# One adaLN block on one core: modulation and Q,K weights loaded without doubled rows, the late modulation in groups of four tiles, another written-out order

## The chip, the cores and the metric

One core of a Trainium2 chip runs the whole program. The metric is the device time of one execution in microseconds (us), the median of several. TensorE (PE) multiplies matrices; VectorE (DVE), ScalarE (ACT) and GpSimd (POOL) work elementwise; SyncE (SP) issues most DMA transfers, ACT a few. Each engine takes its instructions in the order in which the program lists them for it, and waits on semaphores for the others.

## What is computed

x has 2048 rows of 448. Six vectors come from c; then an attention with 16 heads of 28 over a sliding window of 256 rows, and a gated MLP with a mixing over the rows:

```
mod = (silu(c) @ w_mod).reshape(1, 6, 1, 448)         # sa, ca, ga, sb, cb, gb
h = layernorm(x) * (1 + ca) + sa
q, k, v = split(h @ wqkv)                              # 16 heads of 28
p = softmax(where(0 <= i - j < 256, q k^T * 28**-0.5, -1e9))
x = x + ga * ((p v) @ wo)
h = layernorm(x) * (1 + cb) + sb
z = gelu(h @ w_in); z1 = z[:, :896]; z2 = layernorm(z[:, 896:])
x = x + gb * ((z1 * (w_sp @ z2 + b_sp)) @ w_out)
```

## The kernel before

The 2048 rows are 16 tiles of 128. The 448 features lie in four chunks of 128 that start at 0, 128, 192 and 320 (`CH`), so features 192 to 255 stand in chunk 1 and in chunk 2. `load_dup` (L481) loads a weight to match: rows 0 to 255 into chunks 0 and 1, rows 192 to 447 into chunks 2 and 3, which is 512 rows for 448. The doubled rows must count once: for Q and K a memset (`z_qk`, L528) zeroes the lower 64 partitions of chunk 2, for the modulation a zero in the row of c (`z_c`, L539) does it.

Every step is an operation with a name, made by `P.op`. The text ORDER lists all operations by their place in that list; a number may carry a PSUM bank choice (after a slash) and an engine choice (after a dot). `schedule` (L81) takes them in that order, and `emit` (L115) writes each engine's instruction stream from it, with the semaphore waits that follow from the data, from a buffer's last users and from the PSUM banks. So ORDER sets every engine's order, SP's and ACT's transfers among them. The names used below, in order of work:

- Loads: `c`; `x0`, `x0b`, `x1` to `x4` (tiles 0; 1; 2-3; 4-7; 8-11; 12-15); `wmodA` (columns of sa and ca); `wqk` (Q and K columns); `wv`; `wmodG` (ga); `woq0` to `woq2` (wo).
- Start: `silu0` loads ACT's first table, `c_cols` turns c into columns, `silu` makes `sc_sb`, `modA` are 16 pairs of one-column matmuls, and `modAe` (DVE, L574) puts sa and 1+ca into `modT`. `warm` are 22 matmuls without use.
- First LayerNorm: `l1_t st0` and `ag` are the statistics of tile t (DVE, L589, L592), `ve`, `rs` (POOL, L597) and `nm` its scale and shift, `xn t` the normalized tile. Tiles are taken in blocks: block 0 is tile 0, block 1 tile 1, block 2 tiles 2-3, blocks 3 to 5 four tiles each. Blocks 0 to 2 are transposed by PE (`tr`), and `hT b_u` (L673 on ACT, L678 on DVE) applies `modT` while it empties the bank; blocks 3 to 5 go through DMA transposes (`hx t`, L695) and four modulating operations each (`hm b_c`, L687).
- Q and K weights: heads of 28 columns are spread to 32 by `wqkf0_c`, `wqkf1_c` (c the chunk, 0 or 1 for the first or second half of the heads; L710 to L712). `qk b_g` are the projections, four matmul steps each, g 0 to 3 for Q and 4 to 7 for K; in block 0 four of the eight read the unspread weights (`mm_heads`, L751). `qke b_g` empties them (L783 ACT, L786 DVE); `v t` and `ve t` are the same for V (L795, L798).
- Attention of tile j: `S j_u` scores, `E j_u` the exponential of 1024 columns (ACT, L885), `M j_u` the mask (POOL, L891), `PV j_u`, `oq`, `rec`, `nrm`, `oT` (L917 to L926), `wo j`, and `x1_j` adds to x (L936). For tile 0 the scores come in two halves, `S0_0h0` and `S0_0h2`, each with two pairs of banks: (0,1),(2,3) and (4,5),(6,7). `E0_0` and `E0_1` read them.
- Second LayerNorm: `l2_j` as above in pairs of tiles, `x2_j` (L610), DMA transpose `h2T j`, and four modulating operations of 256 columns per pair, `h2m j_c` (L945 to L957).
- MLP: `z2m t` and `z1m tb_f` are the projections with w_in. Five tiles (0 to 4) are done early: `z2e` copies them (L983, L986) and `z2g` applies gelu later; the others go through gelu directly (`z2g`, `z1g`). `l3` and `z2n` normalize z2. `G` multiplies with w_sp (loaded transposed, `wsp`), `ga`, `gu`, then `out`, `fin` and the store `st`.

The S of tile j+1 is listed ahead of the PV of tile j, and the PSUM banks 0 to 5 rotate in pairs among the S. The last `E15_5` comes after `z1g0_5`, `z1g0_4` and `z2g7`.

## Time and profile before

| | us |
|---|---|
| median of 3 runs | 271.01 (270.79 to 271.61) |
| profiled execution | 270.71 |
| its span in the trace | 268.7 |
| PE busy | 256.8 (96%) |
| DVE busy | 172.5 (64%) |
| ACT busy | 133.3 (50%) |
| POOL busy | 106.6 (40%) |

The span runs from the first instruction to the last; the execution's time has 2.0 us more around it. In the timeline a row has start, duration, engine, line, operation, tiles, shape, count, and in brackets the idle time of the engine before it with what ended it. Rows of the same kind in sequence are merged, and then the duration is that of all of them with the small gaps between. ACT operations overlap, so 60 E of 1044 ns stand in 55.80 us.

### The profile page before, as it was taken

What the parts mean: (1) busy time and instruction counts of PE and PEld (TensorE: products, weight loads), DVE (VectorE), ACT (ScalarE), POOL (GpSimd) and SP (SyncE); (2) the same over time, 40 slices, a digit from 0 to 9 for tenths busy, and PEclk for the clock granted to TensorE, in tenths of its full rate; (3) what the DMA queues carried; (4) which work ended last, traced back from release to release, by engine and by line L of the source; (5) the groups of instructions that cost most, each with busy time, mean ns of one, the idle gap of its engine ahead of it and who ended that gap; (6) DMA issues with size and microseconds to landing.
All of it is one profiled execution on the core that took longest, in us unless ns stands there. A gap on an engine that the chain in (4) does not pass through costs nothing.

```text
span 268.7 us, 7296 instructions
## 1 busy us (share of the span) xinstructions
PE 256.8 (96%) x3139; PEld 127.5 (47%) x3161; DVE 172.5 (64%) x402; ACT 133.3 (50%) x180; POOL 106.6 (40%) x170
## 2 busy tenths in 40 slices
...
GB/s 225 358 211 47 61 115 120 110 5 41 234 194 77 81 46 76 65 77 156 135 159 192 202 183 113 0 2 0 0 0 2 0 0 34 53 35 0 0 54 103
DMA packets 60861, 23.96 MB, mean 89 GB/s; under 512 B 49822, under 2 KB 60701, under 8 KB 60829
## 3 DMA queue, kind: packets, MB, share of 16 engines
...
## 4 chain that ended last, share of the span: by engine, by line
PE 81%; ACT 8%; DVE 7%; DMA 2%; issue 1%; SPq 0%; DVEq 0%
PE ps L457 72%; PE ps L454 8%; ACT PT L885 7%; DMA x_sb<-in_A_x_dram 2%; DVE st_all L589 1%; DVE hT L687 1%; DVE w_out_sb L941 1%; DVE hT L678 1%; DVE oq L917 1%; DVE x_sb L936 0%; DVE z L983 0%; DVE nm_all L627 0%; SPq L484 0%; ACT xn L640 0%; DVE o_sb L922 0%
## 5 line engine op out<-in xcount | busy, mean ns | idle before, releaser
L885 ACT ACTIVATE PT<-ps 128x1024 bf16<-128x1024 f32 x90 | 84.6, 1044 | 2.9 <-PE ps L457 2.8
L1081 DVE TENSOR_TENSOR tmpg<-ps,bsp_bc 128x512 bf16<-128x512 f32 x28 | 19.2, 690 | 56.0 <-PE ps L457 55.8
L457 PE MATMUL ps<-QKT,z 128*128 128x512 bf16 x221 | 49.8, 379 | 0.2
L1012 ACT ACTIVATE z1T<-ps 128x512 bf16<-128x512 f32 x28 | 15.4, 596 | 67.0 <-PE ps L457 66.8
L891 POOL TENSOR_SCALAR_AFFINE_SELECT PT<-PT 128x512 f32<-128x512 f32 x60 | 37.8, 646 | 7.7 <-ACT PT L885 7.5
L457 PEld LDWEIGHTS ps<-QKT,z 128*128 128x128 bf16 x224 | 21.9, 98 | 26.2
L597 POOL TENSOR_TENSOR rs_all<-ve_all,neghalf 128x1 f32<-128x1 f32 (+2 forms) x30 | 19.9, 667 | 28.7 <-DVE ve_all L596 28.7
L457 PE MATMUL ps<-w_spC,z 128*128 128x512 bf16 x107 | 24.9, 379 | 0.3
L457 PE MATMUL ps<-w_spD,z 128*128 128x512 bf16 x110 | 24.6, 379 | 0.1
L457 PE MATMUL ps<-w_in_sb,hT 128*128 128x448 bf16 (+1 forms) x103 | 22.5, 353 | 0.7 <-DVE hT L687 0.4
L457 PE MATMUL ps<-w_out_sb,z1T 128*128 128x448 bf16 (+2 forms) x119 | 22.3, 341 | 0.0
L589 DVE BATCH_NORM_STATS2 st_all<-x_sb 128x6 f32<-128x448 bf16 x32 | 19.4, 612 | 3.1 <-DMA x_sb<-in_A_x_dram 2.7
L457 PE MATMUL ps<-hT,w_in_sb 128*128 128x512 bf16 (+1 forms) x88 | 21.2, 380 | 0.1
L457 PE MATMUL ps<-QKT 28*128 28x128 bf16 x720 | 18.3, 217 | 1.6 <-DVE hT L678 0.6
L786 DVE CAST QKT<-ps 128x512 bf16<-128x512 f32 (+2 forms) x28 | 17.2, 616 | 3.4 <-PE ps L457 1.9
L589 DVE BATCH_NORM_STATS2 st_all<-z2raw 128x6 f32<-128x448 bf16 x32 | 18.7, 611 | 0.6 <-ACT z2raw L993 0.6
L687 POOL TENSOR_SCALAR hT<-hT,modT 128x256 bf16<-128x256 bf16 (+1 forms) x28 | 17.6, 636 | 3.3 <-DMA hT<-xn 3.3
L457 PE MATMUL ps<-hT,WQK 128*128 128x128 bf16 (+2 forms) x108 | 17.2, 298 | 1.3 <-issue 0.6
L610 POOL TENSOR_SCALAR xn<-x_sb,rs_all,nm_all 128x512 bf16<-128x512 bf16 x21 | 17.0, 815 | 2.7 <-DVE nm_all L601 1.9
L457 PEld LDWEIGHTS ps<-QKT 28*128 28x128 bf16 x720 | 10.5, 92 | 15.2 <-ACT PT L885 10.2
L1103 DVE TENSOR_TENSOR fin<-ps,x_sb 128x448 bf16<-128x448 f32 (+2 forms) x17 | 10.0, 596 | 11.9 <-PE ps L457 7.8
L457 PEld LDWEIGHTS ps<-w_spC,z 128*128 128x128 bf16 x112 | 10.9, 98 | 13.2
...
## 6 DMA issues: line engine op xcount, KB each, us to landing
...
x_sb<-in_A_x_dram SPq DMA_DIRECT2D x3, 448.0 KB, 8.4
...
wmod_sb<-in_w_mod_dram SPq DMA_DIRECT2D x1, 448.0 KB, 4.4
wmod_sb<-in_w_mod_dram ACTq DMA_DIRECT2D x1, 448.0 KB, 4.9
```

Of the source, the lines that this page charges most:

```text
L454: last = e.matmul(out_[32 * j:32 * j + 32], lhsT=lhsT[:, 32 * j:32 * j + 32], rhs=rhs, start=st, stop=sp, tile_position=(0, 32 * j), **kw)
L457: return e.matmul(out_, lhsT=lhsT, rhs=rhs, start=st, stop=sp, **kw)
L589: st = [dve("%sst%d" % (name, i), prio, dve_ns(D), lambda e, i=i, s_=s_: e.bn_stats(st_all[:, slot, t, i, :], s_()), deps, tens) for i, s_ ...
L597: r = pool(name + "rs", prio, 420 + 148 * n, lambda e: e.tensor_tensor(rs_all[:, slot, t0:t1], ve_all[:, slot, t0:t1], neghalf[:, t0:t1], ...
L610: return e.tensor_scalar(dst, src, rs_all[:, slot, t:t + 1], nm_all[:, slot, t:t + 1], ALU.mult, ALU.add)
L687: return e.tensor_scalar(hT[:, c_, cols], hT[:, c_, cols], modT[:, base_col + 4 + c_:base_col + 5 + c_], modT[:, base_col + c_:base_col + ...
L786: return e.tensor_copy(QKT[:, g, cols], ps[:, ten.slot, 0:w])
L885: e_op = P.op("E%d_%d" % (j, ui), pr, [("act", 925, lambda e, e_in=e_in, e_out=e_out: e.activation(e_out(), e_in(), ACT.Exp, scale=SCALE)) ...
L891: ready = pool("M%d_%d" % (j, ui), pr - 50, pool_ns(512), lambda e, pt=pt, pat=pat, cm=cm, cmp=cmp: e.affine_select(out=pt32(pt.slot), in_ ...
L1012: g = P.op("z1g%d_%d" % (tb, ft), pr - 19, [("act", act_ns(512), lambda e: e.activation(z1T[:, ft, tb * 512:(tb + 1) * 512], ps[:, ten.slo ...
L1081: a = dve("ga%d_%d" % (tb, ft), pr, dve_ns(512), lambda e, tb=tb, ten=ten, tg=tg: e.tensor_tensor(tmpg[:, tg.slot, :], ps[:, ten.slot, :], ...
L1103: fs.append(dve("fin%s%d" % (nm, t), pr, dve_ns(c1 - c0), lambda e, t=t, ten=ten, ft_=ft_, c0=c0, c1=c1: e.tensor_tensor(fin[:, ft_.slot, ...
```

## The change

The modulation weights come in four transfers: rows 0-255 of both vectors (`wmodA01`, SP), rows 320-447 (`wmodA3`, ACT), and rows 256-319 of sa and of ca each as a transfer of 64 rows into the lower and the upper half of chunk slot 2 (`wmodAR0`, `wmodAR1`, ACT). `sc_sb` gets a fifth column, so that one matmul with c in the lower or the upper 64 partitions and zeros in the others reads the half that it needs. The Q,K weights come as `wqk03` (rows 0-127 and 320-447), `wqkM` (rows 128-255 for Q, 192-319 for K) and two 64-row rests (`wqkR0`: rows 128-191 for K; `wqkR1`: rows 256-319 for Q). The spread weights are made by three full copies per half (`wqkf0_0`, `0_3`, `0_M`, and with 1) and two of 64 partitions (`wqkr`), and two memsets (`zwq0`, `zwq1`) zero the unused halves once. The projections take their chunks in the order 0, 3, 1, 2 instead of 2, 3, 0, 1. The second half of tile 0's scores may use the banks (0,1),(2,3) too. The second LayerNorm takes tiles 0-3, 4-7 and 8-11 in groups of four, with modulating operations of 512 columns (`h2q`), and 12-13 and 14-15 in pairs; what reads h2 waits for its group.

The order is another one throughout. Written out by name, the parts that matter here (before, then after):

```
SP     x0 wmodA0 wqk1 x0b x1 wqk0 x2 wv0 wmodG1 wv1 woq0 x3 woq1 wmodG0 x4 woq2 hx4 hx7 hx6 hx5 hx8 ...
SP     x0 wmodA01 wqk03 x0b x1 wqkR0 wqkR1 wqkM x2 wv0 x3 wmodG1 woq2 wv1 woq1 wmodG0 woq0 hx6 hx4 hx7 hx5 x4 hx8 ...
ACT    c wmodA1 silu0 silu exp0 wqkf1_3 wqkf0_3 hT0_3 hT0_0 hT0_1 xn1 qke0_4 qke0_1 qke0_5 hT1_1 E0_0 ... E0_1 ve0 qke1_7 hT2_1 E1_1 E1_0 qke2_0 qke2_1 E1_2 E1_3 qke2_6 E2_0 E2_1 ve3 E2_2 E2_3 ve2 qke3_0 E2_5 E2_4 ve7 E3_0 E3_1 qke3_1 E3_3 ... E13_1 z2e0_0 E13_3 E13_2 z2e1_0 E13_4 ... E15_4
ACT    c silu0 wmodA3 wmodAR0 wmodAR1 silu exp0 wqkf0_0 wqkf1_3 wqkf0_3 wqkr0_k wqkr0_q hT0_0 hT0_3 wqkr1_q hT1_1 qke0_5 qke0_4 qke0_0 qke0_1 qke0_2 wqkr1_k qke1_5 E0_0 ... E0_1 qke1_7 hT2_1 E1_0 E1_1 ve0 qke2_2 qke2_3 E1_2 E1_3 qke2_7 qke2_4 qke2_6 E2_0 E2_1 qke2_5 ve2 E2_2 E2_3 qke3_0 E2_4 E2_5 qke3_2 E3_1 E3_0 E3_2 E3_3 qke3_3 E3_4 ... E14_3 z2e2_0 E14_5 E14_4 ve15 E15_0 ... E15_4
DVE    xn0 l1_1st0 l1_1ag modAe l1_1ve hT0_2 l1_2st0 l1_1nm l1_3st0 ... hT1_0 ... hT2_0 l1_4nm xn4
DVE    xn0 zwq1 zwq0 l1_1st0 l1_1ag l1_1ve l1_3st0 l1_3ag l1_1nm l1_2st0 modAe l1_2ag hT0_2 hT0_1 hT1_0 ... l1_4nm xn6 hT2_0
POOL   l1_0rs zqk wqkf1_2 l1_1rs wqkf0_2 wqkf1_0 l1_2rs wqkf0_0 wqkf0_1 xn2 zv ...
POOL   l1_0rs wqkf1_0 l1_1rs xn1 wqkf0_M wqkf1_M l1_2rs xn3 xn2 l1_4rs ... M15_3 l2_12rs nrm15 h2q8_1 h2q8_2 h2q8_3 h2q8_0
PE     ... modA ... warm20 [qk0: 16 steps] tr1 warm21 S0_0h0 [qk1, qk0: 31 steps] tr2_0 [13 steps] S0_0h2 v0 ...
PE     ... modA ... warm21 tr1 [qk0: 20 steps] [qk1: 8 steps] S0_0h0 [qk1, qk0: 32 steps] S0_0h2 tr2 ...
```

The diff without the list of numbers:

```
--- before
+++ after
@@ ORDER: the whole list is replaced @@
...
@@ -347,7 +346,7 @@
-    sc_sb, _, _ = alloc("sc_sb", [128, 4], BF16)
+    sc_sb, _, _ = alloc("sc_sb", [128, 8], BF16)
@@ -393,7 +392,7 @@
-    crz, _, _ = alloc("crz", [128, 512], BF16, at=e_)
+    crz, _, _ = alloc("crz", [128, 576], BF16, at=e_)
@@ -490,12 +489,24 @@
-    t_wmA = load_dup("wmodA", -98, wmod_sb, w_mod, 0, 2 * D, engs=("sp", "act"), rate=290.0)
-    t_wmA[0].order = [x0]
-    t_wmA[1].order = [t_c]
-    t_wqk = load_dup("wqk", -97, wqk_raw, A_wqkv, 0, 904, order=t_wmA)
-    t_wqk[0].order = [t_wqk[1]]
-    x0b = load_x("x0b", -96, 1, 1, [t_wqk[1]])
+    def dram(v, dims):
+        return bass.AP(v.tensor, v.offset, dims)
+    MW, QW = 6 * D, 3 * D
+    t_wmA = [load("wmodA01", -98, lambda e: e.dma_start(wmod_sb[:, 0:2, 0:2 * D], w_mod[0:256, 0:2 * D].rearrange("(c p) n -> p c n", p=128)),
+                  256 * 2 * D * 2, order=[x0]),
+             load("wmodA3", -98, lambda e: e.dma_start(wmod_sb[:, 3, 0:2 * D], w_mod[320:448, 0:2 * D]), 128 * 2 * D * 2, order=[t_c], eng="act")]
+    t_wmAR = [load("wmodAR%d" % v, -98, lambda e, v=v: e.dma_start(wmod_sb[64 * v:64 * v + 64, 2, 0:D], w_mod[256:320, v * D:(v + 1) * D]), 64 * D * 2, eng="act")
+              for v in range(2)]
+    t_wmAR[0].order = [t_wmA[1]]
+    t_wmAR[1].order = [t_wmAR[0]]
+    t_wmA += t_wmAR
+    t_w03 = load("wqk03", -97, lambda e: e.dma_start(wqk_raw[:, 0:2, :], dram(A_wqkv[0:1, 0:1], [[QW, 128], [320 * QW, 2], [1, 904]])), 256 * 904 * 2, order=[t_wmA[0]])
+    t_wM = load("wqkM", -97, lambda e: e.dma_start(wqk_raw[:, 2, :].rearrange("p (a n) -> p a n", a=2),
+                dram(A_wqkv[128:129, 0:1], [[QW, 128], [64 * QW + D, 2], [1, 452]])), 128 * 904 * 2, order=[t_w03])
+    t_wR = [load("wqkR%d" % g, -97, lambda e, g=g: e.dma_start(wqk_raw[64 * g:64 * g + 64, 3, 0:452], A_wqkv[(128, 256)[g]:(192, 320)[g], (D, 0)[g]:(D, 0)[g] + 452]),
+                 64 * 452 * 2, order=[t_w03]) for g in range(2)]
+    t_wR[1].order = [t_wR[0]]
+    x0b = load_x("x0b", -96, 1, 1, [t_w03])
@@ -525,22 +536,22 @@
-    z_qk = P.op("zqk", -67, [("dve", 480, lambda e: e.memset(wqk_raw[0:64, 2, :], 0.0)), ("pool", 600, lambda e: e.memset(wqk_raw[0:64, 2, :], 0.0))], [t_wqk[1]])
+    z_wq = [P.op("zwq%d" % i, -67, [("dve", 300, lambda e, v=v: e.memset(v, 0.0))])
+            for i, v in enumerate((WQK[0:64, 2, 0:16, :], WQK[64:128, 1, 16:32, :]))]
...
-        for k in range(4):
-            last = mm(e, ps[:, tc_ten.slot, k:k + 1], crz[0:1, 128 * k:128 * k + 128], one[0:1, 0:1], True, True)
+        for k, a in enumerate((0, 128, 256, 448, 320)):
+            last = mm(e, ps[:, tc_ten.slot, k:k + 1], crz[0:1, a:a + 128], one[0:1, 0:1], True, True)
...
-    z_c = dve("zc", -75, 120, lambda e: e.memset(crz[0:1, 256:320], 0.0))
+    z_c = dve("zc", -75, 120, lambda e: e.memset(crz[0:1, 256:512].rearrange("p (a b) -> p a b", b=128)[:, :, 0:64], 0.0))
...
-            dve("cz1", -62, 180, lambda e: e.tensor_copy(crz[0:1, 320:512], crow[0:1, 256:448]), [t_c])]
+            dve("cz1", -62, 180, lambda e: e.tensor_copy(crz[0:1, 320:384], crow[0:1, 256:320]), [t_c]),
+            dve("cz2", -62, 180, lambda e: e.tensor_copy(crz[0:1, 448:576], crow[0:1, 320:448]), [t_c])]
...
-    t_sc = P.op("silu", -59, [("act", 180, lambda e: e.activation(sc_sb[:], ps[:, tc_ten.slot, 0:4], ACT.Silu))],
+    t_sc = P.op("silu", -59, [("act", 180, lambda e: e.activation(sc_sb[:, 0:5], ps[:, tc_ten.slot, 0:5], ACT.Silu))],
@@ -562,15 +573,16 @@
-    for h in (1, 0):
+    for h in (0, 1):
...
-                for kc in (2 * h, 2 * h + 1):
-                    last = mm(e, ps[:, mA_ten.slot, col:col + 1], wmod_sb[:, kc, i * D + CH[mc]:i * D + CH[mc] + 128], sc_sb[:, kc:kc + 1],
-                              h == 1 and col == 0 and kc == 2, h == 0 and kc == 1, skip_group_check=True)
+                for kc, sc in (((0, 0), (1, 1)), ((3, 3), (2, 4 if i == 0 else 2)))[h]:
+                    a = CH[mc] + (0 if kc == 2 else i * D)
+                    last = mm(e, ps[:, mA_ten.slot, col:col + 1], wmod_sb[:, kc, a:a + 128], sc_sb[:, sc:sc + 1],
+                              h == 0 and col == 0 and kc == 0, h == 1 and kc == 2, skip_group_check=True)
...
-            m1.append(pe("modA%d_%d%s" % (col // 4, col % 4, "h" if h else ""), -50, 52, fn, [t_wmA[h], t_sc], [mA_ten], order=m1[-1:], mode=WHOLE))
+            m1.append(pe("modA%d_%d%s" % (col // 4, col % 4, "h" if h else ""), -50, 52, fn, [t_wmA[1:] if h else t_wmA[0], t_sc], [mA_ten], order=m1[-1:], mode=WHOLE))
@@ -699,18 +711,26 @@
-    t_wqkp = [[], []]
+    t_wqkp = []
...
-        for c_ in range(4):
-            src = wqk_raw[:, c_, 224 * gp:224 * gp + 4]
-            src = bass.AP(src.tensor, src.offset, [list(src.ap[0]), [D, 2], [DH, 8], [1, 32]])
-            dst = WQK[:, c_, 8 * gp:8 * gp + 4, :]
-            dst = bass.AP(dst.tensor, dst.offset, [list(dst.ap[0]), [512, 2], [32, 8], [1, 32]])
-            t_wqkp[gp].append(P.op("wqkf%d_%d" % (gp, c_), -45 + gp * 10, [
-                ("dve", 205, lambda e, d=dst, s_=src: e.tensor_copy(d, s_)),
-                ("act", act_ns(512), lambda e, d=dst, s_=src: e.activation(d, s_, ACT.Copy)),
-                ("pool", 620, lambda e, d=dst, s_=src: e.tensor_copy(d, s_))], [t_wqk[c_ // 2]] + ([z_qk] if c_ == 2 else []), port=True))
-    raw_users = sum(t_wqkp, [])
+        def spread_w(name, rows, slot, a, kq, kk, dep, gp=gp):
+            src = wqk_raw[rows, slot, 224 * gp:224 * gp + 1]
+            dst = WQK[rows, kk if kq is None else kq, (16 if kq is None else 0) + 8 * gp, 0:1]
+            src = bass.AP(src.tensor, src.offset, [list(src.ap[0])] + ([] if a is None else [[a, 2]]) + [[DH, 8], [1, 32]])
+            dst = bass.AP(dst.tensor, dst.offset, [list(dst.ap[0])] + ([] if a is None else [[1024 * (kk - kq) + 512, 2]]) + [[32, 8], [1, 32]])
+            n = 256 if a is None else 512
+            return P.op("%s%d_%s" % (("wqkr", "wqkf")[a is not None], gp, name), -45 + gp * 10, [
+                ("dve", 205, lambda e: e.tensor_copy(dst, src)),
+                ("act", act_ns(n), lambda e: e.activation(dst, src, ACT.Copy))] +
+                ([] if a is None else [("pool", 620, lambda e: e.tensor_copy(dst, src))]), [dep], port=True)
+        full = slice(0, 128)
+        c0 = spread_w("0", full, 0, D, 0, 0, t_w03)
+        c3 = spread_w("3", full, 1, D, 3, 3, t_w03)
+        cm = spread_w("M", full, 2, 452, 1, 2, t_wM)
+        ck = spread_w("k", slice(0, 64), 3, None, None, 1, t_wR[0])
+        cq = spread_w("q", slice(64, 128), 3, None, 2, None, t_wR[1])
+        t_wqkp.append(({0: c0, 3: c3, 1: cm, 2: [cq, z_wq[0]]}, {0: c0, 3: c3, 1: [ck, z_wq[1]], 2: cm}, [c0, c3, cm, ck, cq]))
+    raw_users = t_wqkp[0][2] + t_wqkp[1][2]
@@ -751,8 +771,7 @@
-            last = e.matmul(out_[32 * j:32 * j + 32], lhsT=lhsT[:, DH * j:DH * j + 32], rhs=rhs, start=st, stop=sp,
-                            tile_position=(0, 32 * j))
+            last = e.matmul(out_[32 * j:32 * j + 32], lhsT=lhsT[j], rhs=rhs, start=st, stop=sp, tile_position=(0, 32 * j))
@@ -763,22 +782,28 @@
-            for k in (2, 3, 0, 1):
+            for k in (0, 3, 1, 2):
...
-                    e, ps[:, ten.slot, 0:n_], stat(k), mov(k), k == 2, k == 1), [deps[k], hT_op[b][k]], [ten], order=ops[-1:], mode=mode))
+                    e, ps[:, ten.slot, 0:n_], stat(k), mov(k), k == 0, k == 2), [deps[k], hT_op[b][k]], [ten], order=ops[-1:], mode=mode))
...
+                wdeps = t_wqkp[u // 2][g // 4]
...
-                    ops, ten = chain("qk%d_%d" % (b, g), p_, {0: t_wqk[0], 1: t_wqk[0], 2: [t_wqk[1], z_qk], 3: t_wqk[1]},
-                                     lambda k, g=g: wqk_raw[:, k, 112 * g:112 * g + 116], lambda k: hT[:, k, cols], w, COLS, mm_heads)
+                    def raw(k, g=g):
+                        if k == (2 if g < 4 else 1):
+                            return [WQK[:, k, 4 * g + j, :] for j in range(4)]
+                        a = 112 * g + (4 if g >= 4 and k in (1, 2) else 0)
+                        return [wqk_raw[:, {0: 0, 3: 1}.get(k, 2), a + DH * j:a + DH * j + 32] for j in range(4)]
+                    rest = 2 if g < 4 else 1
+                    ops, ten = chain("qk%d_%d" % (b, g), p_, {0: t_w03, 3: t_w03, 3 - rest: t_wM, rest: wdeps[rest]}, raw,
+                                     lambda k: hT[:, k, cols], w, COLS, mm_heads)
...
-                    ops, ten = chain("qk%d_%d" % (b, g), p_, t_wqkp[u // 2], lambda k, g=g: WQK[:, k, 4 * g:4 * g + 4, :].rearrange("p a b -> p (a b)"),
+                    ops, ten = chain("qk%d_%d" % (b, g), p_, wdeps, lambda k, g=g: WQK[:, k, 4 * g:4 * g + 4, :].rearrange("p a b -> p (a b)"),
@@ -856,7 +881,7 @@
-                halves = [[Ten(banks((a, a + 1))) for a in a_] for a_ in ((0, 2), (4, 6))] if j == 0 else [tens]
+                halves = [[Ten(banks((0, 1))), Ten(banks((2, 3)))], [Ten(banks((4, 5), (0, 1))), Ten(banks((6, 7), (2, 3)))]] if j == 0 else [tens]
@@ -942,19 +967,21 @@
-    for j0 in range(0, NT, 2):
-        pr = j0 + 2.0 + G["l2"]
-        ags = [ln_stats("l2_%d" % j, pr, 1, j, [lambda j=j: x_sb[:, j, :]], [x1_op[j]]) for j in (j0, j0 + 1)]
-        rs = ln_rs("l2_%d" % j0, pr, 1, j0, 2, ags, True)
-        for j in (j0, j0 + 1):
+    for j0, n in ((0, 4), (4, 4), (8, 4), (12, 2), (14, 2)):
+        pr = j0 + n + G["l2"]
+        js = range(j0, j0 + n)
+        ags = [ln_stats("l2_%d" % j, pr, 1, j, [lambda j=j: x_sb[:, j, :]], [x1_op[j]]) for j in js]
+        rs = ln_rs("l2_%d" % j0, pr, 1, j0, n, ags, True)
+        for j in js:
...
-        ms = [modulate("h2m%d_%d" % (j0, c_), pr + 0.1, c_, slice(j0 * 128, (j0 + 2) * 128), 256, 8, [h2_raw[j0], h2_raw[j0 + 1]] + t_modB) for c_ in range(4)]
-        h2_op[j0] = h2_op[j0 + 1] = ms
+        ms = [modulate("h2%s%d_%d" % ("mq"[n > 2], j0, c_), pr + 0.1, c_, slice(j0 * 128, (j0 + n) * 128), 128 * n, 8, [h2_raw[j] for j in js] + t_modB) for c_ in range(4)]
+        for j in js:
+            h2_op[j] = ms
@@ -999,7 +1026,7 @@
-            h2d = [h2_op[4 * tb], h2_op[4 * tb + 2], t_win]
+            h2d = [h2_op[4 * tb + i] for i in range(4)] + [t_win]
@@ -1024,7 +1051,7 @@
-                h2p = [h2_op[4 * tb - 4], h2_op[4 * tb - 2], t_win]
+                h2p = [h2_op[4 * tb - 4 + i] for i in range(4)] + [t_win]
...

```

119 lines of the change are left out of this document (59 added, 60 removed).

## The prediction

> **What bounds the kernel now.** I read the stretches first (columns: stretch, its length, then busy us of PE, PEld, DVE, ACT, POOL, the clock, the DMA share, GB/s).
>
> ```profile
> 8.00:10.00 2.00, 1.95 (x52) 1.44 (x53) 1.97 (x7) 1.75 (x5) 1.94 (x4) 1.00 1.07 384
> 10.00:12.00 2.00, 1.36 (x49) 0.81 (x41) 1.97 (x10) 1.88 (x6) 1.46 (x4) 1.00 1.09 380
> 12.00:14.00 2.00, 1.71 (x30) 1.64 (x31) 2.00 (x6) 2.00 (x5) 1.80 (x4) 1.00 1.14 257
> 14.00:16.00 2.00, 1.38 (x22) 1.06 (x19) 1.94 (x9) 1.80 (x11) 1.21 (x2) 1.00 1.03 294
> ...
> 60.00:80.00 20.00, 19.55 (x476) 10.47 (x480) 17.26 (x39) 19.88 (x23) 17.60 (x27) 1.00 0.74 149
> ...
> 100.00:120.00 20.00, 19.28 (x385) 9.45 (x375) 16.83 (x40) 17.02 (x21) 11.59 (x19) 1.00 0.42 69
> ...
> 170.00:200.00 30.00, 29.84 (x138) 13.58 (x140) 12.49 (x24) 0.00 (x0) 0.00 (x0) 1.00 0.00 1
> ```
>
> There are three regimes. Until about 16 us PE has holes (1.55 us between 10 and 16) while DVE has none. In the attention ACT is full. From about 110 us PE runs alone: 138 matmuls in 29.84 us, 216 ns each. The last regime is the same work in both kernels, so the end moves as far as the end of the attention moves. ACT's own timeline shows where the attention loses time:
>
> ```profile
> 16.38 1.02 ACT L885 ACTIVATE PT<-ps 128x1024 bf16<-128x1024 f32 x1 [0.56 <-PE ps L457]
> ...
> 24.17 1.94 ACT L885 ACTIVATE PT<-ps 128x1024 bf16<-128x1024 f32 x2 [0.34 <-PE ps L457]
> ...
> 26.72 1.94 ACT L885 ACTIVATE PT<-ps 128x1024 bf16<-128x1024 f32 x2 [0.17 <-PE ps L457]
> ...
> 32.25 1.94 ACT L885 ACTIVATE PT<-ps 128x1024 bf16<-128x1024 f32 x2 [0.29 <-PE ps L457]
> ...
> 34.85 55.80 ACT L885 ACTIVATE PT<-ps 128x1024 bf16<-128x1024 f32 x60 [0.17 <-PE ps L457]
> 90.86 0.54 ACT L986 ACTIVATE z<-ps 128x448 bf16<-128x448 f32 x1 [0.22 <-PE ps L457]
> ...
> 93.32 0.55 ACT L986 ACTIVATE z<-ps 128x448 bf16<-128x448 f32 x1
> ...
> 101.72 1.94 ACT L885 ACTIVATE PT<-ps 128x1024 bf16<-128x1024 f32 x2 [0.51 <-PE ps L457]
> 103.89 1.94 ACT L885 ACTIVATE PT<-ps 128x1024 bf16<-128x1024 f32 x2 [0.23 <-PE ps L457]
> 106.34 1.02 ACT L885 ACTIVATE PT<-ps 128x1024 bf16<-128x1024 f32 x1 [0.51 <-PE ps L457]
> ```
>
> The first row is `E0_1`; from there ACT hardly rests. It waits 0.97 us between 24 and 35 and 1.25 us between 101 and 107, both for PE. One link of the chain of waits that ended last, just ahead of `E0_1`, and the timeline of the start say why it is no earlier:
>
> ```profile
> 15.08 0.91 DVE hT L678 x2
> ```
>
> ```profile
> 1.80 1.28 ACT L531 ACT_TABLE_LOAD   x1 [1.80 <-issue]
> ...
> 3.07 3.59 PE L457 MATMUL ps<-warm 128*128 128x512 bf16 x8
> ...
> 6.88 0.48 PE L457 MATMUL ps<-warm 128*128 128x512 bf16 x2
> ...
> 7.73 0.63 DVE L589 BATCH_NORM_STATS2 st_all<-x_sb 128x6 f32<-128x448 bf16 x1 [2.70 <-DMA x_sb<-in_A_x_dram]
> ...
> 7.96 1.25 PE L457 MATMUL ps<-warm 128*128 128x256 bf16 x10
> ...
> 8.49 0.13 DVE L574 TENSOR_TENSOR modT<-ps,zero_one 128x8 f32<-128x8 f32 x1
> ...
> 8.61 0.15 DVE L596 TENSOR_SCALAR ve_all<-mv_all 128x1 f32<-128x1 f32 x1
> ...
> 9.26 1.29 PE L754 MATMUL ps<-hT,wqk_raw 128*32 128x128 bf16 x64
> ...
> 9.46 1.17 POOL L712 COPY WQK<-wqk_raw 128x512 bf16<-128x512 bf16 x2
> 9.55 0.54 DVE L627 SCALAR_TENSOR_TENSOR nm_all<-mv_all,rs_all 128x1 f32<-128x1 f32 x1
> ...
> 12.29 1.98 PE L457 MATMUL ps<-hT,WQK 128*128 128x128 bf16 x31 [0.42 <-ACT hT L673]
> ...
> 16.03 0.29 PE L457 MATMUL ps<-QKT 28*128 28x128 bf16 x8 [0.60 <-DVE hT L678]
> ...
> 16.85 1.30 SPq L695 DMA_TRANSPOSE hT<-xn  x1
> ```
>
> PE was through with the projections at 15.43, and `S0_0h2` (16.03) waited 0.60 us for `hT2_0`, which holds one of its banks until DVE empties it.
>
> **The change part by part.** *Loads.* The modulation columns are 784 KB instead of 896, Q and K 791 instead of 904. What gates DVE is `x0b` (the wait of 2.70 us). Ahead of it now stand 112 KB less; at 384 GB/s that is 0.30 us, so 7.43. The Q,K saving lies behind it. `l1_3st0` needs `x1`, 224 KB behind `x0b`, 0.6 us later: 8.0. `wmodA3` and the rests are now issued behind ACT's table load, so from 3.1 at the latest (1.80 + 1.28), three in a row, the last near 4.
>
> ```profile
> wmod_sb<-in_w_mod_dram ACTq DMA_DIRECT2D x1, 448.0 KB, 4.9
> ...
> x_sb<-in_A_x_dram SPq DMA_DIRECT2D x3, 448.0 KB, 8.4
> ```
>
> With 4.9 us to landing they are there by 8.9. That is before `modAe` gets its turn (below), so I cost the late issue at nothing; once that spare us is gone it counts in full. `x4` now waits in SP's queue behind four transposes. From 16.85 on four at 1.30 bring its issue to 22; at the 8.4 us of its kind it would land at 30.4. DVE wants it after `oq1`:
>
> ```profile
> 28.52 0.67 DVE L917 STREAM_TRANSPOSE oq<-ps 128x512 f32<-128x512 f32 x1
> ```
>
> That is 29.2 before, earlier now, with every evacuation of `qk3` queued behind it: a stall of 0 to 2 us. The 8.4 was measured in a full queue; after 20 us the queue is nearly empty, so I take 0. `woq0` moves behind `wmodG0`, but `wog` waits for the gate matmul anyway.
>
> *Zeros and spreading.* POOL loses a memset and two copies; DVE's two memsets fit into its 2.70 us of waiting. The four `wqkr` on ACT are new; each lies between nothing and a full copy's 0.6. Two stand in ACT's wait for `modAe`, two ahead of `E0_0`, which is not what sets `E0_1`: nothing. One more copy and one more one-column matmul for c are hidden by the loads.
>
> *DVE's order.* `modAe` (8.49 before) now stands behind `l1_3st0`, `ag`, `nm` and `l1_2st0`. From 7.43: 0.88 to `ve` (8.61 - 7.73), 0.1, then 0.55, 0.1, 0.15 and 0.55 (statistics every 0.55: 9.00 to 9.55 in the same timeline), so it starts at 9.76 and ends at 9.89, 1.27 later than before (8.62). `nm` took 0.54 in that row while POOL copied; at that price it is 10.3. [...]
>
> *PE's order.* Before, the first projection started 0.64 after `modAe` ended (9.26). So it starts now at 10.53, with tile 1 ready too. Sixty chain steps precede `S0_0h2` in both lists: 16 in 1.29 us, 44 at 1.98/31 = 64 ns make 2.8; the two halves of S take 0.29 each. That gives 15.2, against 16.32 for the end of `S0_0h2` before: no `hT2` is in the way, as the second half takes banks that `E0_0` has read. Gain 1.1 without any wait; before, the holes were 1.55. I take 0.3 of waits back: **-0.8 us** (bounds -1.1 and, below, +0.7).
>
> *ACT's list.* From `E0_1` to tile 3 ACT gets three more `qke2`, one more `qke3` and two fewer `ve`:
>
> ```profile
> L783 ACT ACTIVATE QKT<-ps 128x512 bf16<-128x512 f32 x2 | 1.2, 600 | 0.0
> L783 ACT ACTIVATE QKT<-ps 128x256 bf16<-128x256 f32 x3 | 1.2, 395 | 0.0
> L795 ACT ACTIVATE Vaug<-ps 128x448 bf16<-128x448 f32 x4 | 2.2, 550 | 0.0
> L687 POOL TENSOR_SCALAR hT<-hT,modT 128x256 bf16<-128x256 bf16 x22 | 13.0, 598 | 3.3 <-DMA hT<-xn 3.3
> L687 POOL TENSOR_SCALAR hT<-hT,modT 128x512 bf16<-128x512 bf16 x6 | 4.6, 777 | 0.0
> L922 POOL TENSOR_TENSOR o_sb<-oq,rec_all 128x448 bf16<-128x448 f32 x11 | 10.4, 949 | 3.6 <-DVE rec_all L918 3.2 <-DVE nm_all L627 0.4
> ```
>
> 3 x 0.395 + 0.6 - 2 x 0.55 = +0.69 us, which can go into the 0.97 us that ACT waited: between -0.28 and +0.69. I take **0**, since PE's work there is unchanged. Near the end two `z2e` (0.54 and 0.55) leave tile 13; one `z2e` and one `ve` come in tiles 14 and 15, where ACT waited 1.25 us. If PE keeps up, that is 1.1 us, if not 0. DVE takes over two `z2e`, so I take half: **-0.5 us**.
>
> *Groups of four.* 512 columns cost 777 ns on POOL, two times 256 cost 1196; POOL, at most 11.59 of 20 us busy here, is not the bound: 0. A group waits for its last tile. The tightest is tiles 8-11: on POOL `nrm15` (0.95) and four `h2q8` (3.1) follow `PV15`, plus about 2 on DVE, 6.1 us; PE has 33 matmuls of 0.21, 6.9 us, before it needs them. The cover is 0.8 us.
>
> Sum: -0.8 - 0.5 = -1.3 on the profiled 270.71, 269.4. The median of before lies 0.3 above its profiled execution, so I say **269.7**.
>
> **The rivals.** *All of it:* no waits at the start (-1.1), ACT's waits filled (-0.3), the end in full (-1.1): 271.0 - 2.5 = 268.5. For it speaks that PE has holes in both places; against it, that lists rarely run without new waits.
>
> *A wash:* the start is earlier by 0.8, but ACT's 0.7 more takes its place as the bound until tile 4, and the end gives 0.3: 270.6. For it: ACT at 19.88 of 20. Against: the waits were PE's.
>
> *The late modulation decides (slower):* `modAe` is 1.27 later. If the holes stay as they were, all of PE's list shifts: projections through at 16.7, so `E0_1` 0.7 later than before, `x4` or ACT's extra work adds half of 0.7, and DVE gives nothing back at the end: 272.1. It decides once `E0_1` starts after 16.38. For it: DVE is full from 8 to 16 us and every hT and statistic queues on it.
>
> *The bytes don't matter:* of the loads only 0.30 us is on the path. That the lighter loads alone make the kernel faster I hold for wrong; the gain is from order and banks.
>
> *PE slows down:* eight warm-up matmuls took 3.59 us (449 ns) from 3.07, two from 6.88 took 0.48 (240). Before, they filled PE to 9.21; now PE waits between them and `tr1` (about 10.1). If it falls back for another 3.8 us at half rate, 1.9 us are lost: 271.6. [...]
>
> **How the numbers follow.** All of it 0.14, the forecast 0.36, the wash 0.18, PE slower 0.05, the late modulation 0.27. What can be told from no change is 0.3% (0.8 us): 270.2 to 271.8. Faster 0.50, within 0.23, slower 0.27. The likeliest case alone spans 269.1 to 270.2; with the others and an `x4` stall the range is 268.4 to 272.3.
>
> **What would show it.** Right: `x0b`'s wait ends near 7.4, `modAe` near 9.8, `S0_0h2` no longer waits for DVE, `E0_1` starts at 15.2 to 15.9, and the exponential before the gelu table starts 1 to 1.6 us earlier. Wrong: `E0_1` after 16.4, an ACT wait over 0.6 us in tiles 0 to 4, a PE wait on `hT` L687 near 120 us, or matmuls of 128 columns over 100 ns apart after 10 us.

## The result, and the profile after

| | before | after |
|---|---|---|
| median of nine runs each | 271.17 (270.64 to 271.74) | 272.94 (272.12 to 275.08) |
| ratio | | 1.0073, 95% interval 1.0044 to 1.0102 |
| profiled execution, its span | 270.71, 268.7 | 272.38, 270.7 |
| end of the last matmul in the trace | 265.82 | 265.68 |

The change made the kernel 0.7% slower; 269.7 was predicted. The last row tells where to look: PE ends 0.15 us earlier than before, and the span is 2.0 us longer. So the loss stands behind the last matmul, and what the change gained up to there is small. PE's last rows, of before and then of after:

```profile
253.72 12.10 PE L457 MATMUL ps<-w_out_sb,z1T 128*128 128x448 bf16 x70
```

```profile
251.85 6.80 PE L456 MATMUL ps<-w_out_sb,z1T 128*128 128x192 bf16 x42
258.88 6.79 PE L456 MATMUL ps<-w_out_sb,z1T 128*128 128x448 bf16 x35 [0.23 <-DVE fin L1130]
```

(Three of the nine runs of after, 273.8 to 275.08, had a mean granted clock of 0.988 to 0.991; that has a cause of its own, below. The profiled execution had 1.00 throughout PE's work.)

The groups of instructions on DVE, one row of each kernel, before and then after (busy us, mean ns of one, idle time ahead and what ended it). An addition `fin` adds x to the product and writes one of four `fin` buffers; the store reads it.

```profile
L1103 DVE TENSOR_TENSOR fin<-ps,x_sb 128x448 bf16<-128x448 f32 (+2 forms) x17 | 10.0, 596 | 11.9 <-PE ps L457 7.8 <-DMA out_dram<-fin 4.0
```

```profile
L1130 DVE TENSOR_TENSOR fin<-ps,x_sb 128x448 bf16<-128x448 f32 (+2 forms) x17 | 9.7, 594 | 20.6 <-PE ps L456 10.8 <-DMA out_dram<-fin 9.8
```

The work is the same, but the waits on a store rose from 4.0 to 9.8 us. DVE's timeline at the end, before and then after (start, duration, operation, count, in brackets the wait):

```profile
263.48 1.90 DVE L1103 TENSOR_TENSOR fin<-ps,x_sb 128x448 bf16<-128x448 f32 x4 [2.31 <-DMA out_dram<-fin]
265.86 0.62 DVE L1103 TENSOR_TENSOR fin<-ps,x_sb 128x448 bf16<-128x448 f32 x1 [0.48 <-PE ps L457]
```

```profile
255.27 0.62 DVE L1130 TENSOR_TENSOR fin<-ps,x_sb 128x448 bf16<-128x448 f32 x1 [0.52 <-PE ps L456]
258.20 0.96 DVE L1130 TENSOR_TENSOR fin<-ps,x_sb 128x448 bf16<-128x448 f32 x2 [2.30 <-DMA out_dram<-fin]
260.62 1.16 DVE L1130 TENSOR_TENSOR fin<-ps,x_sb 128x448 bf16<-128x448 f32 x2 [1.46 <-DMA out_dram<-fin]
263.02 0.62 DVE L1130 TENSOR_TENSOR fin<-ps,x_sb 128x448 bf16<-128x448 f32 x1 [1.25 <-PE ps L456]
265.43 1.16 DVE L1130 TENSOR_TENSOR fin<-ps,x_sb 128x448 bf16<-128x448 f32 x2 [1.78 <-DMA out_dram<-fin]
267.84 0.62 DVE L1130 TENSOR_TENSOR fin<-ps,x_sb 128x448 bf16<-128x448 f32 x1 [1.25 <-DMA out_dram<-fin]
```

Before, the last addition follows the last matmul at once. After, it starts 2.16 us behind the last matmul, and from 258.20 on the rows come 2.4 us apart. The buffer numbers in the order say why. After the change `fin11`, `fin14`, `fin10`, `fin8`, `fin3` and `fin5` all take buffer 0. Each must wait until the store of the one before has landed, and a link is 0.62 us of addition and 1.7 of store (the page's median from issue to landing).

Up to the last matmul the two kernels differ little. This is ACT's timeline after, beside the rows of before in the prediction and two more of before:

```profile
15.57 1.03 ACT L910 ACTIVATE PT<-ps 128x1024 bf16<-128x1024 f32 x1
...
18.24 1.94 ACT L910 ACTIVATE PT<-ps 128x1024 bf16<-128x1024 f32 x2 [0.56 <-PE ps L456]
...
94.51 1.94 ACT L910 ACTIVATE PT<-ps 128x1024 bf16<-128x1024 f32 x2 [0.74 <-PE ps L456]
96.95 1.94 ACT L910 ACTIVATE PT<-ps 128x1024 bf16<-128x1024 f32 x2 [0.51 <-PE ps L456]
98.96 0.54 ACT L1013 ACTIVATE z<-ps 128x448 bf16<-128x448 f32 x1
...
106.19 1.02 ACT L910 ACTIVATE PT<-ps 128x1024 bf16<-128x1024 f32 x1 [0.56 <-PE ps L456]
```

```profile
19.07 1.95 ACT L885 ACTIVATE PT<-ps 128x1024 bf16<-128x1024 f32 x2
...
106.34 1.02 ACT L885 ACTIVATE PT<-ps 128x1024 bf16<-128x1024 f32 x1 [0.51 <-PE ps L457]
```

`E0_1` starts 0.81 us earlier (15.57 for 16.38) and the next exponential 0.83 (18.24 for 19.07). The exponential ahead of gelu starts only 0.15 earlier. Counted by the how-manieth exponential ends, after is ahead of before by 0.84 us at the 3rd, 0.42 at the 33rd, 0.54 at the 74th (the last ahead of the first `z2e` of before), 1.92 at the 77th, where before has done its two `z2e`, and 0.14 behind at the 83rd.

### The profile page after: what moved, and what is told of

It reads as the page before. It is cut to its first block, busy times and chain, and to the rows that moved or that the text cites. A ratio compares the mean times of both kernels' runs of the same rounds, so it can differ in the third digit from the quotient of the medians.

```text
span 270.7 us, 7088 instructions
## 1 busy us (share of the span) xinstructions
PE 259.3 (96%) x3057; PEld 127.8 (47%) x3057; DVE 167.2 (62%) x395; ACT 133.2 (49%) x182; POOL 101.6 (38%) x158
## 3 DMA queue, kind: packets, MB, share of 16 engines
HBM read 9.36 MB, written 1.84 MB: 41 GB/s over the span
## 4 chain that ended last, share of the span: by engine, by line
PE 86%; DVE 4%; DMA 4%; ACT 3%; issue 1%; POOL 1%; SPq 0%; DVEq 0%
PE ps L456 79%; PE ps L453 7%; ACT PT L910 2%; DMA out_dram<-fin 2%; DMA x_sb<-in_A_x_dram 2%; DVE fin L1130 1%; DVE st_all L601 1%; DVE oq L942 1%; DVE x_sb L961 0%; DVE w_out_sb L966 0%; POOL o_sb L947 0%; DVE hT L699 0%; ACT hT L685 0%; POOL xn L622 0%; ACT QKT L808 0%
## 5 line engine op out<-in xcount | busy, mean ns | idle before, releaser
L456 PE MATMUL ps<-QKT,z 128*128 128x512 bf16 x224 | 49.0, 379 | 0.0
L916 POOL TENSOR_SCALAR_AFFINE_SELECT PT<-PT 128x512 f32<-128x512 f32 x60 | 37.2, 648 | 4.7 <-ACT PT L910 4.6
L609 POOL TENSOR_TENSOR rs_all<-ve_all,neghalf 128x1 f32<-128x1 f32 (+2 forms) x27 | 18.0, 671 | 34.0 <-DVE ve_all L608 34.0
L456 PE MATMUL ps<-hT,w_in_sb 128*128 128x512 bf16 (+1 forms) x103 | 25.0, 380 | 0.0
L456 PE MATMUL ps<-hT,WQK 128*128 128x512 bf16 (+2 forms) x125 | 22.3, 312 | 0.0
L622 POOL TENSOR_SCALAR xn<-x_sb,rs_all,nm_all 128x512 bf16<-128x512 bf16 x25 | 19.1, 771 | 5.7 <-DVE nm_all L639 2.8
L811 DVE CAST QKT<-ps 128x512 bf16<-128x512 f32 (+2 forms) x25 | 15.7, 626 | 2.9 <-PE ps L456 1.3
L456 PEld LDWEIGHTS ps<-w_spD,z 128*128 128x128 bf16 x112 | 11.0, 98 | 13.2
```

The costliest lines, as they stand in the source:

```text
L456: return e.matmul(out_, lhsT=lhsT, rhs=rhs, start=st, stop=sp, **kw)
L609: r = pool(name + "rs", prio, 420 + 148 * n, lambda e: e.tensor_tensor(rs_all[:, slot, t0:t1], ve_all[:, slot, t0:t1], neghalf[:, t0:t1], ...
L622: return e.tensor_scalar(dst, src, rs_all[:, slot, t:t + 1], nm_all[:, slot, t:t + 1], ALU.mult, ALU.add)
L811: return e.tensor_copy(QKT[:, g, cols], ps[:, ten.slot, 0:w])
L916: ready = pool("M%d_%d" % (j, ui), pr - 50, pool_ns(512), lambda e, pt=pt, pat=pat, cm=cm, cmp=cmp: e.affine_select(out=pt32(pt.slot), in_ ...
```

## The experiments

All are variants of the two kernels. The small order edits are given by operation names. Times are medians with their range; a ratio is against runs of before on the same chip. "Under 0.995" counts runs whose mean granted clock was below that; of the 110 runs of before that went beside these experiments there is none. Runs at 0.999 or 1.000 are called undisturbed below.

| kernel | median (range), runs | ratio, 95% interval | under 0.995 |
|---|---|---|---|
| e1: after, buffers in turn | 270.04 (269.25 to 272.67), 12 | 0.9969, 0.9945 to 0.9993 | 5 |
| e2: before, one buffer | 275.63 (275.30 to 275.78), 4 | 1.0165, 1.0146 to 1.0184 | see text |
| e3: e1, v0 first | 269.79 (269.43 to 272.50), 12 | 0.9965, 0.9943 to 0.9988 | 4 |
| e4: e1, more PE | 271.49 (270.63 to 273.18), 10 | 1.0015, 0.9997 to 1.0032 | 1 |
| e5: e1, more ACT | 270.62 (269.77 to 271.98), 10 | 0.9995, 0.9976 to 1.0013 | 4 |
| e6: e1, fewer warm-ups | 271.89 (270.38 to 273.75), 12 | 1.0028, 1.0002 to 1.0054 | 12 |
| e7: after, other end | 269.76 (268.83 to 272.16), 12 | 0.9966, 0.9940 to 0.9991 | 5 |
| e8: e6 and e7 | 271.99 (271.48 to 273.54), 9 | 1.0041, 1.0017 to 1.0065 | 9 |
| e9: e7, more warm-ups | 269.60 (268.82 to 271.23), 12 | 0.9951, 0.9935 to 0.9968 | 1 |
| e10: e7, early modulation | 269.79 (269.43 to 272.02), 6 | 0.9955, 0.9942 to 0.9968 | 1 |
| e11: e7, gate copied | 269.97 (269.24 to 271.61), 12 | 0.9961, 0.9945 to 0.9977 | 2 |
| e12: e10 and e11 | 269.94 (269.27 to 270.99), 12 | 0.9960, 0.9944 to 0.9975 | 4 |
| e13: before, fewer warm-ups | 272.11 (270.81 to 274.80), 12 | 1.0041, 1.0014 to 1.0067 | 2 |
| e14: after, more warm-ups | 272.16 (271.75 to 274.57), 10 | 1.0046, 1.0024 to 1.0067 | 1 |

### One buffer at the end: e1 and e2

```
- fin14/0  fin8/0  fin3/0  fin9/1  fin5/0
+ fin14/2  fin8/3  fin3/1  fin9/0  fin5/2
```

> The changed kernel with the buffers of five output tiles renamed, so that the last additions take the four fin buffers in turn instead of buffer 0 six times; nothing else moves. Theory 'one buffer': after the last matmul (265.69 us in the changed kernel, 265.84 in the kernel before) the end waits for a chain of store and addition through buffer 0, 2.4 us a link. Then the waits of fin on out_dram go from 9.8 us to under 1, the last addition follows the last matmul as before, and the time falls by 2.0 to 270.9 (ratio to before 0.998 to 1.001). Rival 'the late modulation and the extra work of ACT cost it': the end moves by less than 0.5 and the time stays at 272.5 or above.

DVE's timeline at the end of e1:

```profile
262.89 0.62 DVE L1130 TENSOR_TENSOR fin<-ps,x_sb 128x448 bf16<-128x448 f32 x1 [0.70 <-PE ps L456]
264.21 0.62 DVE L1130 TENSOR_TENSOR fin<-ps,x_sb 128x448 bf16<-128x448 f32 x1 [0.70 <-PE ps L456]
265.54 0.62 DVE L1130 TENSOR_TENSOR fin<-ps,x_sb 128x448 bf16<-128x448 f32 x1 [0.70 <-PE ps L456]
```

Each of these additions waits for PE alone, and the span is 268.4, 2.3 less; the medians lie 2.9 apart (272.94 and 270.04). PE gains too, since an addition that waits holds the PSUM bank that the next outputs need (in after PE waits 0.23 us for `fin` at 258.88): the last 77 output matmuls take 13.42 us for the 13.83 of after (251.85 to 265.68).

```profile
252.08 13.42 PE L456 MATMUL ps<-w_out_sb,z1T 128*128 128x192 bf16 x77
```

Five numbers in the order turned a kernel that was 0.7% slower into one that is 0.3% faster than before. (The waits on a store fell to 3.0, not under 1; the two that are left stand ahead of these rows.) The rival, that the start costs it, falls. The reverse edit in the kernel before:

```
- fin14/2 st4 ... fin7/1 ... st14 fin13/1 ... fin6/2
+ fin14/0 st4 st14 ... fin7/0 ... fin13/0 ... fin6/0
```

> The kernel before with the reverse: fin14, fin7, fin13 and fin6 take buffer 0 like fin12 and fin5, and st14 and st13 stand right behind what they need. Theory 'one buffer': six additions in a chain of 2.4 us from about 256.6, so the last ends near 269.3 instead of 266.5, and the time rises by 2 to 3 us, to 273.1 to 274 (ratio 1.008 to 1.011). Rival (the end isn't bound by the buffers): within 0.3 us of before.

```profile
263.43 0.62 DVE L1103 TENSOR_TENSOR fin<-ps,x_sb 128x448 bf16<-128x448 f32 x1 [2.27 <-DMA out_dram<-fin]
265.83 0.89 DVE L1103 TENSOR_TENSOR fin<-ps,x_sb 128x448 bf16<-128x448 f32 x2 [1.78 <-DMA out_dram<-fin]
268.24 0.95 DVE L1103 TENSOR_TENSOR fin<-ps,x_sb 128x448 bf16<-128x448 f32 x2 [1.52 <-DMA out_dram<-fin]
270.66 0.62 DVE L1103 TENSOR_TENSOR fin<-ps,x_sb 128x448 bf16<-128x448 f32 x1 [1.46 <-DMA out_dram<-fin]
```

The same chain with the same 2.4 us a link, and 4.6 us in the median: more than the 2 to 3 expected, since the chain starts later than I had counted and the last addition ends at 271.28, 2.0 us behind the 269.3 of the expectation. (The mean clock of these runs is 0.991 to 0.995; in the profile it falls at 268.9 us, when PE has ended.)

### A stop inside S1_0: e3

PE's timeline after, where `S1_0` is 16 matmuls that need nothing but what is there:

```profile
17.00 0.39 PE L456 MATMUL ps<-QKT 28*128 28x128 bf16 x13
17.96 0.23 PE L456 MATMUL ps<-QKT 28*128 28x128 bf16 x3 [0.57 <-issue]
```

PE stops between its 13th and 14th matmul with no semaphore to wait for. It costs 0.79 us from start to start, and the exponential behind it is the one that waited 0.56 at 18.24.

```
- v1_2 S1_0 v0_0 v0_3 v0_1 gateA v0_2
+ v1_2 v0_0 v0_3 v0_1 v0_2 S1_0 gateA
```

> As e1, and the four matmuls of v0 stand ahead of S1_0 instead of behind it. In the changed kernel PE stops for 0.79 us inside S1_0, between its 13th and 14th matmul, with no semaphore in the way, after some 450 dense instructions. Theory 'the instructions are late' (the supply of PE's instructions, not data): the 0.75 us of v0 fill that time, S1_0 ends where it did (18.2), no stop is left over 0.3, and PE is 0.6 to 0.75 ahead from there; if PE is the bound from 24 us on, the time falls by 0.5 to 0.7 against e1 (270.3). Rival 'S1_0 itself waits for something': S1_0 ends 0.7 later, near 18.9, and the time is that of e1 or up to 0.5 above.

```profile
17.94 0.67 PE L456 MATMUL ps<-QKT 28*128 28x128 bf16 x16
```

The stop shrank to 0.26, as the first theory says: `S1_0` ends 0.17 later than in e1 and the 0.75 us of `v0` are done by then, so PE is 0.6 ahead. But the undisturbed runs lie where those of e1 do (269.43 to 269.99 and 269.25 to 270.10). PE's lead alone gave nothing: `E1_0` started 0.16 later (18.65 for 18.49), and 2 us later PE waits for ACT, which it doesn't in e1:

```profile
20.64 0.40 PE L456 MATMUL ps<-QKT 28*128 28x128 bf16 x16 [0.30 <-ACT PT L910]
```

What goes with the stop can be read over all profiles. The trace has transfers of 16 KB that it calls instruction, one for every 250 or so instructions of PE (24 in after, for 6114 matmuls and weight loads). The first within the span ends at 14.8 to 17.2 us, between the loads.

| profile | transfer ends | PE goes on within S1_0 | difference | stop |
|---|---|---|---|---|
| after | 16.40 | 17.96 | 1.56 | 0.79 |
| e1 | 16.67 | 18.21 | 1.54 | 0.79 |
| e3 | 16.73 | 18.32 | 1.59 | 0.26 |
| e12 | 16.39 | 17.90 | 1.51 | 0.27 |
| e4 | 15.54 | S1_0 runs through from 17.11 | | none |
| e9 | 15.21 | S1_0 runs through from 17.32 | | none |

In after, e1, e3 and e12 PE came there earlier, and stood until 1.51 to 1.59 us behind the transfer's end; in e4 and e9 it began `S1_0` 1.57 and 2.11 us behind it and ran through. So the times fit the first theory, that PE's instructions are late. That the transfer brings them is an inference from its label and these times, and what sets the time of the transfer is not shown, as no run changed the loads.

### Which engine bounds the attention: e4 and e5

```
- put(step k)
+ put(step k), twice for the first step of each qk4 (start and stop set, then start)
```

> As e1, with the first matmul of each of the eight chains qk4 done twice: 8 times 0.216 = 1.7 us more of PE between 35 and 65 us. Theory 'PE is the bound from 24 us to the end' (its records show 100% from 24 to 60 us): the time rises by 1.5 to 1.9 against e1. Theory of the prediction ('in the attention ACT is full', PE has room there): PE takes it from its waits and the time rises by 0 to 0.5.

ACT's last exponential ahead of gelu, in e1 and then in e4:

```profile
106.42 1.02 ACT L910 ACTIVATE PT<-ps 128x1024 bf16<-128x1024 f32 x1 [0.56 <-PE ps L456]
```

```profile
107.34 1.02 ACT L910 ACTIVATE PT<-ps 128x1024 bf16<-128x1024 f32 x1 [0.56 <-PE ps L456]
```

Most of PE's 1.73 us more counts. This profile had no stop in `S1_0`, so up to the 24th exponential it is 0.93 us ahead of e1. The doubled matmuls stand between the 24th and the 43rd, and behind them it is 0.5 behind: 1.4 to 1.5 us of the 1.73. Another 0.4 is lost between the 66th and the 74th, where nothing was added; why is open. The medians are 1.45 us apart, those of the undisturbed runs 1.8.

```
- activation(E of 1024 columns)
+ activation(columns 0 to 511), activation(512 to 1023), for tiles 6 and 8
```

> As e1, with the twelve exponentials of tiles 6 and 8 done in two halves of 512 columns each: more ACT time between 40 and 62 us, about 0.2 us for each split (an exponential of 1024 columns comes every 0.93 us; an estimate from that and from the 0.60 us of a copy of 512 columns), 2.4 us in all, and nothing more for PE. e4 showed that 1.7 us more of PE in this stretch count in full. Theory 'PE and ACT are both full here, so more of either counts and less of one alone gives nothing': the time rises by 1.8 to 2.4 against e1 (to 272 to 272.4). Theory 'PE alone is the bound from 24 us': it rises by less than 0.6.

ACT's timeline of e5, the halves of tile 6 and what follows:

```profile
49.65 5.99 ACT L910 ACTIVATE PT<-ps 128x512 bf16<-128x512 f32 x12
55.38 5.76 ACT L911 ACTIVATE PT<-ps 128x1024 bf16<-128x1024 f32 x6
```

I had the size of the edit wrong. A half of 697 ns (its row among the groups) comes every (5.99 - 0.70) / 11 = 0.48 us, so two cost 0.96, where whole ones that nothing delays start 0.90 apart. A split costs about 0.06 and all twelve 0.7 us, not 2.4. The ends of the exponentials show it: e5 is level with e1 at the 30th, 0.34 behind at the 36th (tile 6 is done), 0.70 at the 48th (tile 8), and 0.55 at the last; the median is 0.58 up. That time, under 0.6, is what the rival expects, since the edit was too small to tell by the median. The exponentials tell: most of ACT's addition counts too. PE and ACT are both full here, and a lead of PE alone, the 0.6 us of e3, gave nothing.

### PE's clock: e6, e7, e8 and e9

```
- for i in range(22):        # warm-ups
+ for i in range(14):
```

> As e1, with 14 warm-up matmuls instead of 22: the last eight go, 16 instructions of PE's list, and what stands at a given place of the list moves up by 16. Theory 'the instructions are late': the stop of 0.6 to 0.8 us inside S1_0 then falls behind S1_0, among the matmuls of v0 (0.19 us each), where most of it is covered; E1_0 follows hT2_1 without a wait of over 0.2, at 17.6 to 17.9, PE and ACT are both ahead by 0.6 to 0.8, and the undisturbed runs fall by 0.5 to 0.8 against those of e1, to 268.8 to 269.2. Rival 'S1_0 waits for data': the stop stays inside S1_0 and the time is that of e1. Third: without the warm-ups PE falls back to a slower pace before tr1 (matmuls of 128 columns over 100 ns apart near 11 us), and the time rises by 1 to 2 us.

The third case came, in all 12 runs. The stretches of e6 (stretch, length, busy us of PE, PEld, DVE, ACT, POOL, the granted clock, DMA share, GB/s):

```profile
8.00:12.00 4.00, 2.07 (x60) 1.85 (x64) 3.83 (x15) 3.52 (x9) 2.64 (x5) 0.58 1.10 353
12.00:16.00 4.00, 4.00 (x75) 3.41 (x65) 2.33 (x7) 3.17 (x10) 2.03 (x3) 0.57 0.85 249
```

e7 has all warm-ups and the end in another order: `out11` instead of `outh15` while the last `ga` runs, buffers in turn, each store behind its addition, and `fin5 st5 fin15 finh15 st15` last.

> The changed kernel with its last 40 operations put in another order: the fin buffers in turn, each store right behind its addition, and the two halves of tile 15 (256 and 192 columns) as the last of all. The chain behind the last matmul then is an addition of 192 columns (about 0.3 us) instead of 448 (0.62): 0.3 us less than e1, 269.7. Rival: the store that ends last is st5 or st9 behind it in SP's queue, and nothing changes against e1.

Its seven undisturbed runs, 268.83 to 269.84, lie 0.3 to 0.4 under those of e1, as the shorter last addition (192 columns, 0.36 us) promises. The profile is one of the other five; these are the stretches ahead of, in and behind its two falls:

```profile
7.47:10.88 3.41, 2.09 (x39) 1.72 (x37) 2.96 (x11) 2.23 (x6) 1.65 (x3) 1.00 1.10 332
10.88:14.29 3.41, 3.41 (x80) 2.86 (x77) 2.89 (x9) 2.94 (x10) 2.67 (x5) 0.50 1.07 327
14.29:17.70 3.41, 3.41 (x62) 2.82 (x62) 2.60 (x12) 3.27 (x10) 1.37 (x2) 1.00 0.33 106
...
89.39:92.80 3.41, 1.89 (x86) 1.32 (x83) 3.25 (x8) 3.41 (x5) 2.65 (x4) 1.00 0.00 0
92.80:96.21 3.41, 3.41 (x10) 1.15 (x8) 1.95 (x6) 1.84 (x3) 3.41 (x6) 0.50 0.26 43
```

PE's timeline of e7 shows where it begins; the row under it is the same work after the change, at full clock:

```profile
10.71 0.46 PE L456 MATMUL ps<-ident,xn 128*128 128x128 bf16 x4 [1.32 <-POOL xn L622]
11.09 0.72 PE L774 MATMUL ps<-hT,wqk_raw 128*32 128x128 bf16 x20
```

```profile
10.45 0.38 PE L456 MATMUL ps<-ident,xn 128*128 128x128 bf16 x4 [1.04 <-POOL xn L622]
10.76 0.46 PE L774 MATMUL ps<-hT,wqk_raw 128*32 128x128 bf16 x20
```

After 1.32 us of waiting for `xn1`, the projections take 0.72 instead of 0.46. The clock stands at 0.50 for 3.41 us and at 1.00 on both sides, so a fall costs 1.7 us of clock (3.41 x 0.50); e7 pays it a second time from 92.80 us, behind the waits of PE at tile 13 (89 to 92 us). One such fall is 1.7 / 270 = 0.006 of the mean clock, two are 0.013: most runs of these kernels stand at 1.000, 0.994 and 0.987.

> e6 and e7 together. If both do what their theories say, 0.8 to 1.1 below e1, 268.6 to 269.2 in undisturbed runs, the lowest so far and 0.8% below before.

e8, with the fewer warm-ups of e6, had no run over 0.994. Then the opposite:

```
- for i in range(22):   n_ = 512 if i < 9 else 256
+ for i in range(27):   n_ = 512 if i < 9 or i > 21 else 256      # five more right ahead of tr1
```

> As e7, with five more matmuls without use (512 columns, 0.22 us each) behind the last warm-up, where PE waits 1.0 to 1.6 us for xn1. e7 and e6 were profiled with a granted clock of 0.5 to 0.86 from 10.7 us on, for 3.4 us and 6 us, and again near 92 us. Theory 'the idle stretch ahead of tr1 lowers PE's clock': the lowered clock at 10 to 17 us is gone; of the runs with a mean clock under 0.995 (7 of 19 of e1 and e7 taken without their profiles, 12 of 12 of e6, which has fewer warm-ups) at most those remain that fall near 92 us (0.994, none at 0.987), and the median falls by 0.2 to 0.5 against e7, to 269.3 to 269.6. Rival 'the lowered clock comes from elsewhere' (the whole chip, the place in the loop): as many runs under 0.995 as in e7, and the median up by 0 to 0.3.

```profile
8.00:12.00 4.00, 2.96 (x69) 2.00 (x73) 3.41 (x13) 3.56 (x10) 2.47 (x5) 1.00 1.09 350
12.00:16.00 4.00, 4.00 (x104) 3.27 (x91) 3.97 (x16) 3.96 (x18) 2.83 (x4) 1.00 0.86 253
```

One run of 12 under 0.995, at 0.993. e9 is the fastest kernel of this study by median: 0.49% under before and 1.2% under after. Its gain over e7 is that fewer runs are disturbed: the undisturbed ones, 268.82 to 270.40, lie no lower than those of e7. In the stretch ahead of the first fall of e7 PE's longest wait is 1.32 us, and it was busy for 2.09 of 3.41 us. So a stretch with little work in it was enough in that run. And the stretches of e7 show more: its two falls start 81.92 us apart, 24 times the 3.41 us that a fall lasts. In e10 they start at 10.74 and 92.66, 24 times as well, in e6 at 8.65 (for two such stretches) and 93.98, 25 times. So the falls of these three profiles lie on a grid of 3.41 us, and the grid is not at the same place in all: counted back, its first line is at 0.6 us in e7, 0.5 in e10 and 1.8 in e6. That fits a light stretch that lowers the clock in some runs only. What sets a fall off stays open. In the stretch ahead of these falls PE is busy for 1.8 to 2.1 of 3.41 us (1.5 in e8). But e5, whose PE waits 1.57 us for `xn1`, has only 1.84 from 9.07 to 12.48, a stretch of the grid of its one fall, at 268.48 behind PE's end, and it keeps its clock.

The two last kernels ask whether it is PE's rest and nothing else of the change. e13 takes eight warm-ups from the kernel before, e14 gives the changed kernel, with its end untouched, the five of e9.

> The kernel before with 14 warm-ups instead of 22, so that PE rests between the last modA (7.9 us) and the first projection (9.3 us) and once more ahead of S0_0h0; nothing of the change is in it. Theory 'an idle stretch of PE in the first 10 us lowers its clock, whatever else the kernel holds': most runs show a mean clock under 0.995 (none of the runs of before does), and the undisturbed rest aside the time rises by 1 to 2 us, to 272 to 273. Rival 'the lowered clock comes with the new loads or the new order of the attention': no run under 0.998, and the time is that of before within 0.3.

> The changed kernel itself, its end untouched, with the five further warm-ups of e9. Theory 'two causes add up in the changed kernel: one buffer at the end in every run (2.3 us), a lowered clock in some runs': the time is 272.0 to 272.5, no run goes over 273.5 (three of nine of the changed kernel did, at clocks of 0.988 to 0.991), and the spread shrinks to 1 us. Rival: the spread stays as it was, with about a third of the runs over 273.5.

e13 has two runs at 0.987 (273.87 and 274.80), where before has none in 110, so the fall can be had without anything of the change. But it is two runs and not most, and the other ten are slower by 0.9 us than before as well, which I can't explain. Its rest is only 0.42 us by its profile. e14 has the expected median, 272.16, but one run of ten over 273.5 where none was expected; after had three of nine. The counts are small; that the rest at the start lowers the clock is shown by e6, e8 and e9 together (12 of 12, 9 of 9 and 1 of 12 runs under 0.995), for the second place, near 92 us, it is seen in three profiles (e6, e7 and e10) and was not removed.

### Two attempts at more: e10, e11 and e12

e10 puts `modAe`, `hT0_2`, `hT0_1` ahead of `l1_2st0` and `tr1` behind twelve steps of the first projections.

> As e7, with modAe, hT0_2 and hT0_1 ahead of l1_2st0 in DVE's list and tr1 behind twelve steps of the first projections in PE's. It takes back a part of what the change did to modAe (1.4 us later than before). Theory 'PE could begin its projections 0.5 to 0.7 earlier and has no hole ahead of tr1': the first projection starts at 10.0 to 10.4 instead of 10.7 to 11.1, E0_1 0.4 to 0.7 earlier; since PE and ACT are both ahead, the undisturbed runs fall by 0.3 to 0.7 to 268.3 to 268.6, and the lowered clock at 10 us becomes rarer. Rival: the stop for instructions, 0.6 to 0.8 us, grows by as much, or E1 waits for hT2 behind later statistics, and the time stays that of e7.

It gained nothing over e7 (undisturbed 269.43 to 270.00). The first projection started at 10.67 all the same: the last 16 `modA` ran at 9.20 behind a wait of 0.85 us for their weights. Those are the 64-row rests that ACT now issues. In the profiles of this family they let the last 16 `modA` start between 8.2 and 9.3; in the kernel before, the last 16 began at 7.5.

e11 copies the gate of w_out out of PSUM, moves its four multiplications to 157 us, and puts three steps of `z2m1` into the waits of PE that the changed kernel has at tile 13:

```profile
89.25 0.40 PE L456 MATMUL ps<-QKT 28*128 28x128 bf16 x16 [0.67 <-ACT PT L910]
91.08 0.40 PE L456 MATMUL ps<-QKT 28*128 28x128 bf16 x16 [0.62 <-ACT PT L910]
```

> As e7, but DVE copies the gate of w_out (448 columns) out of its PSUM bank near 88 us, and the four multiplications with it, 4 us of DVE between 87 and 94, move to 157 us, where DVE rests; h2q0_1 moves from POOL to DVE behind the copy, and three steps of z2m1 into the free bank ahead of and behind S13_2. Theory 'groups of four leave PE without work at tile 13' (PE waits 0.9 and 0.8 us at 88 and 90 us, as nothing that reads h2 is ready): these waits shrink to under 0.4 each, the E of tiles 14 and 15 come 0.4 to 1.0 earlier, and the lowered clock near 92 us is gone (no run at 0.994 from there). Undisturbed runs 0.4 to 1.0 below e7: 268.0 to 268.6. Rival 'ACT is the bound there, the waits of PE cost nothing': the E of tile 14 move by less than 0.3, and the time is that of e7.

A miss as well. ACT's timeline of e11:

```profile
94.45 1.94 ACT L910 ACTIVATE PT<-ps 128x1024 bf16<-128x1024 f32 x2 [0.51 <-PE ps L456]
96.90 1.94 ACT L910 ACTIVATE PT<-ps 128x1024 bf16<-128x1024 f32 x2 [0.51 <-PE ps L456]
99.35 0.54 ACT L1014 ACTIVATE z<-ps 128x448 bf16<-128x448 f32 x1 [0.51 <-PE ps L453]
```

The wait ahead of tile 14 fell from 0.74 to 0.51, and another of 0.51 came at 99.35. ACT had been working without a pause while PE waited (in after from 85.35 to 93.77), so those waits of PE were no loss. e12 joins both and gains as little.

> e10 and e11 together. If both theories hold, undisturbed runs at 267.6 to 268.3 and few or no runs under a mean clock of 0.995: 1.1% below before. If PE's start is eaten by the stop for instructions and ACT is the bound at tile 13, it is e7 within 0.3.

## Why the prediction was wrong

The step that failed is this sentence: "The last regime is the same work in both kernels, so the end moves as far as the end of the attention moves." The matmuls are the same and end within 0.15 us. But the order of the outputs, their buffers and their stores was replaced with the rest, and what stands behind the last matmul is 2.14 us longer than before. With the buffers in turn the span is 2.3 us shorter (e1), and one buffer in the kernel before makes it longer (e2). The buffer numbers stand in the new order; with them, the 0.62 us of `fin` and the store's 1.7 us the chain could have been worked out beforehand. With that one cause taken away the kernel runs in 270.04, near the 269.7 that the other steps gave. That is luck more than a proof of them. The sum had put the whole gain at the end of the attention. There e1's profile is no earlier than before (106.42 for 106.34), and its gain of 0.61 us, 270.10 for 270.71, is 0.32 at the last matmul and 0.3 in the time around the span. In e9, the fastest kernel, 0.31 of 1.28 us (269.43) are gained by the end of the attention. What makes PE's work behind the attention 0.4 us shorter than before in both, no run shows. So a second step failed, the -1.3 at the end of the attention, of which after has 0.15. Part by part:

**Loads.** `x0b` and `modAe`, DVE's timeline after:

```profile
7.57 0.63 DVE L601 BATCH_NORM_STATS2 st_all<-x_sb 128x6 f32<-128x448 bf16 x1 [1.73 <-DMA x_sb<-in_A_x_dram]
...
9.27 0.16 DVE L639 SCALAR_TENSOR_TENSOR nm_all<-mv_all,rs_all 128x1 f32<-128x1 f32 x1
9.35 0.62 DVE L601 BATCH_NORM_STATS2 st_all<-x_sb 128x6 f32<-128x448 bf16 x1
9.88 0.15 DVE L586 TENSOR_TENSOR modT<-ps,zero_one 128x8 f32<-128x8 f32 x1
```

The wait for `x0b` ends at 7.57; 7.43 was expected, 7.73 it was: half the gain. The rests were said to be there by 8.9 and to cost nothing, which held in this profile (8.2), but they come as late as 9.2 in others, so the cover is thin (e10). No stall for `x4` appeared, and none was expected.

**DVE's order.** `modAe` starts at 9.88 for 9.76, and `nm` took 0.16, where the sum had 0.15. That it would be the short one was an estimate: before, 11 of the 13 `nm` took 0.10 to 0.20, and the two long ones (0.54 at 9.55, 0.51 at 12.49) ran beside POOL's copies of the Q,K weights. After, POOL had nothing to do beside it and waited 0.30 us for it. What makes it long, no run shows.

**PE's order.** Right in place and size: `E0_1` started at 15.57, within 15.2 to 15.9, 0.81 earlier. Of this lead 0.54 were left at the 74th exponential. The stop in `S1_0` (0.79 us) kept it from growing: up to the third exponential it grew by 0.05, in e4 and e9, which had no stop, by 0.7, to 1.40 and 1.19 instead of 0.84. Nothing in the prediction allowed for it.

**ACT's list.** The 0.69 us more in tiles 0 to 4 did take part of the lead: ahead 0.84 at the 3rd exponential, 0.42 at the 33rd. The -0.5 at the end was wrong. ACT does get past tile 13 without the two `z2e`, 1.92 ahead at the 77th. But "if PE keeps up" was not met: ACT waited 0.74, 0.51 and 0.56 us for PE in tiles 14 and 15, and had one `z2e` and one `ve` there, and the lead was 0.15 at the end. The reading behind it, "in the attention ACT is full", was half of it: PE is full too (1.4 to 1.5 of 1.73 us more work came through in e4), so moving work off ACT alone did not bring the end forward by more than the 0.15 us. PE's busy time of before did not show this, because some of its records are missing: 221 of the 224 matmuls of one group, for example, against 224 after.

**The rivals.** The late modulation, the slower case that I gave 0.27, did not decide: `E0_1` was early. The wash, which I gave 0.18, comes nearest to what happened up to the last matmul: the lead shrank, to 0.15 us, though not by ACT's work alone. The slower clock, which I gave 0.05, is real: three of the nine runs of the changed kernel have a lowered clock (0.988 to 0.991) and lie 1.2 to 2.5 us above the middle of the other six.

So the profiled 272.38 is 270.71 - 0.15 (PE's end) + 2.14 (behind the last matmul) - 0.32 (the time around the span, 1.73 for 2.05).
